# First attention chunks of a fused kernel: the diagonal bonus and the rounding remainder move to TensorE, the powers of the decay come from one scan

## The chip, the cores and the metric

One core of a Trainium2 chip runs the whole kernel. The metric is the device time of one execution in microseconds (us). The engines are TensorE (PE; PEld is its weight load), VectorE (DVE), ScalarE (ACT), GpSimd (POOL) and SyncE (SP), which here issues most DMAs. Each runs its own instructions in the order in which the program gives them, and waits on semaphores for the others.

## The reference

Three stages follow one another: a linear attention with a decay, a squared-ReLU MLP, and a mixture of experts that routes each token to two of eight. The change touches the first stage and what it hands to the second.

```python
B, H, S, D = r.shape                      # 4, 8, 768, 48
state = zeros(B, H, D, D)
for t in range(S):
    kt, vt, rt = k[:, :, t], v[:, :, t], r[:, :, t]
    cur = einsum('bhd,bhe->bhde', u[None] * kt, vt)
    y[:, :, t] = einsum('bhd,bhde->bhe', rt, state + cur)
    state = w[None, :, :, None] * state + einsum('bhd,bhe->bhde', kt, vt)
x = y.transpose(0, 2, 1, 3).reshape(3072, 384)
h = maximum(x @ w_in, 0); x = (h * h) @ w_out           # 384 -> 2048 -> 384
...
```

## The kernel before, in words

The 3072 tokens go in 24 chunks q of 128; four chunks make one block j of 512 tokens (TPB = 4, six blocks). A chunk of the attention has these steps. `load` brings r, k and v (192 KB each). `p_tr q r` and `p_tr q k` transpose r and k on TensorE, four transposes each, so that the head dimension lies on the partitions; for r, VectorE multiplies by powers of the decay on the way out of the bank (L444), for k of chunks 1 to 7, ScalarE copies (L448), since k was multiplied before (`pre_k`, L408). `pre q` makes r times k times u on GpSimd in two products (L395, L396), and `pre2 q` sums that over a head on VectorE (L414): dg, the bonus of the token itself, one number per token and head. ScalarE then writes am, eight diagonal matrices ident * dg (L419, eight instructions of 128x128). `p_a q` multiplies kT by rT (L459), and VectorE writes the part above the diagonal into am with a predicated copy (L463). `p_kv q` makes the state's update (L503; VectorE adds it to Z at L510, GpSimd multiplies by a power of the decay at L511). `p_y q 0` multiplies the old state, `p_y q 1` multiplies am by v, both into one bank (L477).

`p_x q` hands the chunk over: x1h = the bank rounded to the short fp32 format that TensorE multiplies in one pass (ScalarE, L522), x1l = bank - x1h, the remainder (VectorE, L523). mm1 then multiplies x1h and x1l by the halves of w_in (L540), nine matmuls per slice of 128 hidden units; gsplit squares and splits the result (L545 to L555), mm2 multiplies by w_out (L565, L571). For block 0, slice 0, the terms with x1l come last.

The weights w_in and w_out come in 16 pieces through two staging buffers (`load_w`). Piece n is split by `conv_w1` (ScalarE, L272), `conv_w2` part a and b (VectorE, L279 to L291), and `conv_w3` (ScalarE L301, GpSimd L302); the end of `conv_w2 n` issues the load of piece n+2.

The order of everything up to mm1 of block 0 is written out by hand in the tuple HEAD: each entry is a step, and the engines' queues get their instructions in that order. `warm n` are n transposes of the identity that nothing reads. Behind HEAD, the pieces of chunk 4 and later ones stand at fixed places between the 16 slices of mm1 and mm2 of the block before (CHUNKS: for chunk 4, pre2 at 0.83, p_kv at 1.23, p_y 0 at 1.96, p_a at 3.2, p_y 1 at 5.12; 2f is behind mm1 of slice f). Steps also issue DMAs on SP's queue: `pre q` loads k of q+2, `p_y q 1` v of q+2, `p_tr q k` (of chunk 4: r) r of q+2.

The powers T of the decay (one row per head dimension, centred on the middle of the chunk) are made ahead of HEAD on VectorE: a scan, the reciprocal of its middle column, and a second scan from there (L335 to L340). `tables` reverses them on ScalarE (L344), transposes them on TensorE (L347) and copies them out as tk (L348); `spread` writes u to all partitions by a matmul (L352) and a copy to ub (L354).

Banks of PSUM that the steps use are rings: "att" has three, "ph" two, "xo" one tile of three banks, and a new tile waits for the readers of the oldest released one.

Of the kernel before, what the change touches and what calls it, by code (L numbers as in the profile page):

```python
# [8 lines left out]
F32 = mybir.dt.float32  # L9
F32R = mybir.dt.float32r  # L10
BF = mybir.dt.bfloat16
I32 = mybir.dt.int32
AF = mybir.ActivationFunctionType
OP = mybir.AluOpType
AX = mybir.AxisListType
PSUM = bass.MemoryType.PSUM
DRAM = bass.MemoryType.DRAM
P = 128
# [5 lines left out]
OWN_ACT = 8  # L24
KP_POOL = (2, 3, 4, 5, 6, 7, 8)

HEAD = ("load_w 0", "p_tr 0 r", "spread", "pre 0", "p_tr 0 k", "warm 10", "tables", "pre2 0",
# [7 lines left out]

CHUNKS = (((0.72, 2.09, 0.63, 0.83, 1.23, 3.2, 1.96, 5.12, 6.53),
# [56 lines left out]
def body(ctx, tc, r, k, v, w, u, w_in, w_out, w_gate, w_noise, noise, w1, w2, out):  # L93
    nc = tc.nc
    B, H, S, D = r.shape
    DM = H * D
    FF = w_in.shape[1]
    E, _, F2 = w1.shape
    NT = B * S
    KD = DM // P  # L100
    NF = FF // P
    NF2 = F2 // P
    HP = H // 2
    NCH = NT // P
# [28 lines left out]
    C = {}  # L133
# [25 lines left out]
    ident = consts.tile([P, P], F32, name="ident")  # L159
# [16 lines left out]
    m1 = pool("m1", stack=c_ctx)  # L176
    at = pool("at", side="right", stack=a_ctx)
# [3 lines left out]
    QD = 2 * TPB  # L181
    SRC = {"r": r, "k": k, "v": v}

    def load(q, names="rkv"):
        if q >= NCH:
            return
        b, c = divmod(q, CPB)
        for nm in names:
            if nm in L.get(q, {}):
                continue  # L190
            if nm == "r" and q < QD:
                t = rp[q % 2][:, :, :D]
# [30 lines left out]
    wp = at.tile([P, HP], F32, name="wp")  # L223
# [96 lines left out]
    pb = bank()  # L320
    for _ in range(WARM):
# [5 lines left out]
    s0 = at.tile([P, HP, P], F32, name="s0", tag="rT", bufs=2)  # L327
    s1 = at.tile([P, HP, P], F32, name="s1", tag="rT", bufs=2)
    T = at.tile([P, HP, P], F32, name="pow")
    nc.vector.memset(s1, 0.0)  # L330
    nc.vector.memset(s1[:, :, :1], 1.0)
    nc.vector.tensor_copy(s0, wp[:, :, None].to_broadcast([P, HP, P]))
    nc.vector.memset(s0[:, :, :1], 0.0)
    flat = "p h n -> p (h n)"
    nc.vector.tensor_tensor_scan(T.rearrange(flat), s0.rearrange(flat), s1.rearrange(flat), 0.0,  # L335
                                 op0=OP.mult, op1=OP.add)
    wmid = at.tile([P, HP], F32, name="wmid")
    nc.vector.tensor_tensor(wmid, T[:, :, MID], T[:, :, MID], op=OP.mult)
    nc.vector.reciprocal(s1[:, :, :1], T[:, :, MID:MID + 1])
    nc.vector.tensor_tensor_scan(T.rearrange(flat), s0.rearrange(flat), s1.rearrange(flat), 0.0,  # L340
                                 op0=OP.mult, op1=OP.add)
    def tables():
        Tb = at.tile([P, HP, P], F32, name="back", tag="am", bufs=2)
        nc.scalar.activation(Tb, T[:, :, ::-1], AF.Copy)  # L344
        pb = bank()
        for hp in range(HP):
            nc.tensor.transpose(pb[:, hp * P:(hp + 1) * P], Tb[:, hp, :], ident)  # L347
        nc.scalar.activation(tk, pb.rearrange("p (h x) -> p h x", x=64)[:, :, :D], AF.Copy)  # L348
# [7 lines left out]
    def warm(n):  # L356
        pw = xops.tile([P, KD, BLK], F32, name="xo")
        for _ in range(n):
            nc.tensor.transpose(pw[:, 0, :P], ident, ident)

    Z = [at.tile([P, HP, 2 * D], F32, name=f"Z{i}") for i in range(2)]
    for t in Z:
        nc.gpsimd.memset(t, 0.0)
# [22 lines left out]
    def pre(q):  # L386
        a = A.setdefault(q, {})
        l = L[q]
        if q:
            pre_k(q)  # L390
        if q < QD:
            t = at.tile([P, H, D], F32, name="ra", bufs=2)
        else:
            t = at.tile([P, H, D], F32, name="rk", bufs=1)
        nc.gpsimd.tensor_mul(t, l["r"], l["k"])  # L395
        nc.gpsimd.tensor_mul(t, t, ub)  # L396
        a["rk"] = t
        load(q + 2, "k")
# [8 lines left out]
    def pre_k(q):  # L407
        (nc.gpsimd if q in KP_POOL else nc.vector).tensor_mul(kp[q % 2][:, :, :D], L[q]["k"], tk)  # L408

    def pre2(q):  # L410
        a, l = A[q], L[q]
        t = a["rk"]
        dg = at.tile([P, H], F32, name="dg", bufs=2)
        nc.vector.tensor_reduce(dg, t, axis=AX.X, op=OP.add)  # L414

        a["am"] = at.tile([P, H, P], F32, name="am", tag="am", bufs=2)
        if q < OWN_ACT:
            for h in range(H):
                nc.scalar.activation(a["am"][:, h, :], ident, AF.Copy, scale=dg[:, h:h + 1])  # L419
        else:  # L420
            nc.gpsimd.tensor_mul(a["am"], ident[:, None, :].to_broadcast([P, H, P]),
                                 dg[:, :, None].to_broadcast([P, H, P]))

        nc.gpsimd.tensor_copy(ends(q), pairs(q)[:, :, 32:64].rearrange("p a (s x) -> p a s x", s=2))

    def p_tr(q, which, *tag):
        a = A.setdefault(q, {})
        if q >= QD:
            t = a[which + "T"] = at.tile([P, HP, P], F32, name=which + "T", bufs=2)
            nc.vector.transpose(t.rearrange("p a (s i) -> p a i s", i=TQ),  # L430
                                turned[which].rearrange("p a (i x) -> p a i x", x=D)[:, :, :, :32])
            nc.gpsimd.tensor_mul(t[:KR], t[:KR], T[:KR] if which == "r" else T[:KR, :, ::-1])
            if which == "k":
                load_next(q + 1)
            return
        src = (rp if which == "r" else kp)[q % 2]
        pb = bank(*tag)
        for hp in range(HP):
            nc.tensor.transpose(pb[:KR, hp * P:(hp + 1) * P],
                                src.rearrange("p h x -> p (h x)")[:, hp * P:hp * P + KR], ident)  # L440
        t = at.tile([P, HP, P], F32, name=which + "T", bufs=2)
        src = pb[:KR].rearrange("p (h t) -> p h t", t=P)
        if which == "r":
            nc.vector.tensor_mul(t[:KR], src, T[:KR])  # L444
        elif q == 0:
            nc.vector.tensor_mul(t[:KR], src, T[:KR, :, ::-1])
        else:
            nc.scalar.activation(t[:KR], src, AF.Copy)  # L448
        if which == ("r" if q == TPB else "k"):
            if q + 2 < QD:  # L450
                load(q + 2, "r")
        a[which + "T"] = t

# [61 lines left out]
    def p_x(q, *tag):  # L515
        j, i = divmod(q, TPB)
        if i == 0:
            x1h[j] = m1.tile([P, KD, BLK], F32R, name="x1h", bufs=2)
            x1l[j] = m1.tile([P, KD, BLK], F32R, name="x1l", bufs=2)
        src = A[q]["y"][:, :DM].rearrange("p (d t) -> p d t", t=P)  # L520
        hi = x1h[j][:, :, i * P:(i + 1) * P]
        nc.scalar.activation(hi, src, AF.Copy)  # L522
        nc.vector.tensor_tensor(x1l[j][:, :, i * P:(i + 1) * P], src, hi.bitcast(F32), op=OP.subtract)  # L523
        if q + 1 == QD:
            load_next(QD)
        del A[q], L[q]
# [523 lines left out]
    def run(pieces, n):  # L1050
        for p in pieces[:n]:
# [1 line left out]
        del pieces[:n]  # L1053

    AW = 3
    steps = dict(spread=spread, warm=warm, p_tr=p_tr, pre=pre, tables=tables, pre_k=pre_k, load_w=load_w, p_a=p_a, pre2=pre2, p_kv=p_kv,
                 conv_w1=conv_w1, conv_w2=conv_w2, conv_w3=conv_w3, p_y=p_y, p_x=p_x, load=load)
    for step in HEAD:
        name, *args = step.split()
# [207 lines left out]
```

## Time and profile before

| | us |
|---|---|
| three runs | 954.05, 954.15, 956.12 (median 954.15) |
| the profiled execution | 954.55 |
| its span, first to last instruction | 952.8 |

The profile is of one execution; its times count from the first instruction of the span. A line of a timeline gives start, length, engine, line of the kernel, operation, output <- inputs, and in brackets the idle time ahead of it with what ended it. A line of a group gives the count, the busy time with the mean of one in ns, and the idle time ahead.

### The profile page before, as it was taken

What the parts mean: (1) busy time and instruction counts of PE and PEld (TensorE: products, weight loads), DVE (VectorE), ACT (ScalarE), POOL (GpSimd) and SP (SyncE); (2) the same over time, 40 slices, a digit from 0 to 9 for tenths busy, and PEclk for the clock granted to TensorE, in tenths of its full rate; (3) what the DMA queues carried; (4) which work ended last, traced back from release to release, by engine and by line L of the source; (5) the groups of instructions that cost most, each with busy time, mean ns of one, the idle gap of its engine ahead of it and who ended that gap; (6) DMA issues with size and microseconds to landing.
All of it is one profiled execution on the core that took longest, in us unless ns stands there. A gap on an engine that the chain in (4) does not pass through costs nothing.

```text
span 952.8 us, 17752 instructions
## 1 busy us (share of the span) xinstructions
PE 939.4 (99%) x6845; PEld 805.6 (85%) x6845; DVE 537.5 (56%) x982; ACT 432.7 (45%) x792; POOL 347.3 (36%) x406
## 2 busy tenths in 40 slices
PE   8899999999999999999999999999999999999997
PEld 7676787778778878877888899999989898989986
DVE  8999757635845563584254564554645555456420
ACT  5766655334534434453555542443444434444321
POOL 6665353544463372445030343122121221212112
PEclk9999999999999999999999999999999999999999
DMA  7655379932444271442024357476655555555212
GB/s 176 164 163 163 102 186 302 249 106 68 115 118 105 52 196 44 121 108 77 1 95 97 109 127 185 110 138 133 130 103 114 121 115 110 112 99 109 36 21 37
DMA packets 193233, 112.32 MB, mean 118 GB/s; under 512 B 131777, under 2 KB 185698, under 8 KB 193122
## 3 DMA queue, kind: packets, MB, share of 16 engines
q1 hardware_dynamic: 181698, 91.03, 37.9%
q0 software_dynamic: 10624, 19.74, 11.3%
q8 instruction: 75, 1.23, 0.6%
q14 instruction: 36, 0.29, 0.1%
q10 hardware_dynamic: 800, 0.02, 0.0%
HBM read 74.64 MB, written 36.12 MB: 116 GB/s over the span
## 4 chain that ended last, share of the span: by engine, by line
PE 92%; DVE 4%; DMA 1%; issue 1%; ACT 0%; POOL 0%; POOLq 0%; ACTq 0%; DVEq 0%; SPq 0%
PE ph L540 20%; PE ph L861 19%; PE xo L571 19%; PE y L918 14%; PE y L949 5%; PE att L477 4%; PE ph L949 2%; PE att L459 2%; PE att L604 2%; PE y L861 2%; PE xo L565 1%; PE att L962 1%; PE att L503 1%; DVE am L463 1%; DVE t L280 1%
## 5 line engine op out<-in xcount | busy, mean ns | idle before, releaser
L929 POOL DMA_INDIRECT out<-yt,id x56 | 87.2, 1556 | 297.4 <-ACT yt L927 256.7
L555 DVE TENSOR_TENSOR gl<-g,gh 128x512 fp32r<-128x512 f32 x90 | 77.7, 863 | 134.2 <-ACT gh L553 130.6
L904 DVE SCALAR_TENSOR_TENSOR hl<-ph,hh 128x512 fp32r<-128x512 f32 (+1 forms) x112 | 67.0, 599 | 113.1 <-ACT hh L903 112.2
L545 ACT ACTIVATE rt<-ph 128x512 f32<-128x512 f32 x96 | 57.1, 595 | 158.2 <-PE ph L540 138.5
L540 PE MATMUL ph<-x1h,wih 128*128 128x512 f32 x288 | 119.2, 414 | 0.0
L861 PE MATMUL ph<-xh,w0h 128*128 128x512 f32 (+3 forms) x336 | 118.0, 351 | 0.0
L861 PE MATMUL ph<-xl,w0h 128*128 128x512 f32 (+3 forms) x336 | 116.2, 346 | 0.0
L861 PE MATMUL ph<-xh,w0l 128*128 128x512 f32 (+3 forms) x336 | 116.2, 346 | 0.0
L540 PE MATMUL ph<-x1h,wil 128*128 128x512 f32 x288 | 112.5, 391 | 0.0
L540 PE MATMUL ph<-x1l,wih 128*128 128x512 f32 x288 | 112.2, 391 | 0.0
L571 PE MATMUL xo<-gh,wol 128*128 128x512 f32 x270 | 106.2, 393 | 0.0
L903 ACT ACTIVATE hh<-ph 128x512 fp32r<-128x512 f32 (+1 forms) x112 | 58.7, 525 | 88.9 <-PE ph L861 84.6
L918 PE MATMUL y<-w1h,hh 128*128 128x384 f32 x256 | 85.7, 335 | 0.0
L918 PE MATMUL y<-w1l,hh 128*128 128x384 f32 x256 | 85.6, 335 | 0.0
L918 PE MATMUL y<-w1h,hl 128*128 128x384 f32 x256 | 85.6, 334 | 0.0
L732 POOL DMA_INDIRECT sent<-row,si x48 | 50.2, 1045 | 63.7 <-DVE gl L555 44.8
L571 PE MATMUL xo<-gh,woh 128*128 128x512 f32 x180 | 71.6, 398 | 0.0
L571 PE MATMUL xo<-gl,woh 128*128 128x512 f32 x180 | 70.2, 390 | 0.0
L861 PEld LDWEIGHTS ph<-xh,w0l 128*128 128x128 f32 x336 | 63.2, 188 | 7.7
L861 PEld LDWEIGHTS ph<-xl,w0h 128*128 128x128 f32 x336 | 63.3, 188 | 7.6 <-DVE xl L830 0.8
L861 PEld LDWEIGHTS ph<-xh,w0h 128*128 128x128 f32 x336 | 63.3, 188 | 6.7
L540 PEld LDWEIGHTS ph<-x1h,wih 128*128 128x128 f32 x288 | 54.0, 188 | 16.3 <-issue 3.5
(234 smaller groups left out, 2143.3 us busy)
## 6 DMA issues: line engine op xcount, KB each, us to landing
ws<-in_moe_w SPq DMA_DIRECT2D x128, 96.0 KB
ws<-in_moe_w SPq DMA_DIRECT2D x32, 384.0 KB
sent<-zero SPq DMA_DIRECT2D x8, 1375.5 KB
G<-sent SPq DMA_DIRECT2D x36, 192.0 KB
stg<-in_moe_w_in SPq DMA_DIRECT2D x8, 768.0 KB
stg<-in_moe_w_out SPq DMA_DIRECT2D x8, 768.0 KB
out<-zero SPq DMA_DIRECT2D x5, 960.0 KB
lv<-in_v SPq DMA_DIRECT2D x24, 192.0 KB
```

What stands on the lines that cost most here:

```text
L477: nc.tensor.matmul(pb[32 * n:32 * n + 32, d, :], x, y, skip_group_check=True, **kw)
L540: nc.tensor.matmul(ph, wt[qi][:, d, sl], xt[j][:, d, :], start=(n == 0), stop=(n == 3 * KD - 1))
L545: nc.scalar.activation(rt, ph, AF.Relu)
L555: nc.vector.tensor_tensor(gl, g, gh.bitcast(F32), op=OP.subtract)
L571: nc.tensor.matmul(XO[j][:, d, :], wt[qi][:, fo, sl], gt, start=(f == 0 and n == 0), stop=(f == NF - 1 and n == 2))
L732: st = nc.gpsimd.indirect_dma_start(out=sent, in_=s["row"][:, i, :], in_offset=None, out_offset=bass.IndirectOffsetOnAxis(ap=s["si"][:, i, ...
L861: nc.tensor.matmul(ph[:, c], wt[:, d, sl], xt[:, d, c], start=(m == 0), stop=(m == 3 * KD - 1))
L903: nc.scalar.activation(hh[:, :n], ph, AF.Relu)
L904: nc.vector.scalar_tensor_tensor(hl[:, :n], ph, 0.0, hh[:, :n].bitcast(F32), op0=OP.max, op1=OP.subtract)
L918: nc.tensor.matmul(py, ht[:, sl], wt[:, fo, :], start=(m == 0), stop=(m == 3 * NF2 - 1))
L929: st = nc.gpsimd.indirect_dma_start(out=out, in_=yt, in_offset=None, compute_op=OP.add, out_offset=bass.IndirectOffsetOnAxis(ap=IDX[e, un] ...
L949: nc.tensor.matmul(py[d][:, c], wt[:, fo, sl], ht[:, c], start=(m == 0), stop=(m == 3 * NF2 - 1))
```

## The change

In chunks 1 to 4 (DOT) the bonus no longer comes from r, k and u: `dot q` multiplies kT by rT on GpSimd into rkT, and `pre2 q` multiplies rkT by uw (u times w, two columns per pair of heads) with four matmuls, and ScalarE copies the bank to dg. In chunks 0 to 3 `p_x` lets TensorE subtract x1h from the bank that holds the output (matmul with minus = -identity), and ScalarE copies what is left to x1l. The powers come from one scan, started at the reciprocal of w to the 64th, which six products and a reciprocal make; ScalarE writes the scan's factors. HEAD is put in another order, with `tables` in two parts, fewer `warm` transposes, and u loaded a second time in another layout.

```diff
-HEAD = ("load_w 0", "p_tr 0 r", "spread", "pre 0", "p_tr 0 k", "warm 10", "tables", "pre2 0",
-        "pre_k 0", "conv_w1 0", "pre 1", "p_tr 1 r", "pre2 1", "warm 2", "p_a 0", "p_kv 0",
-        "load 3 r", "load 2 r", "conv_w2 0 a", "p_tr 1 k", "p_y 0 0", "load_w 1", "warm 10",
-        "p_y 0 1", "p_tr 2 r", "pre 2", "p_kv 1", "p_x 0", "p_tr 2 k ph", "pre 3", "pre2 2",
-        "warm 10", "p_a 1", "p_y 1 0", "p_tr 3 r ph", "warm 4", "p_y 1 1", "conv_w2 0 b", "p_kv 2",
-        "p_x 1", "conv_w1 1", "conv_w3 0", "p_tr 3 k ph", "pre2 3", "p_a 2", "conv_w2 1 a",
-        "warm 9", "p_a 3 ph", "pre 4", "p_y 2 0", "p_y 2 1", "p_x 2", "conv_w1 2", "conv_w2 1 b",
-        "p_tr 4 r", "p_y 3 0", "p_kv 3", "p_y 3 1", "p_x 3", "conv_w3 1", "conv_w2 2", "p_tr 4 k")
+DOT = (1, 2, 3, 4)
+HEAD = ("load_w 0", "p_tr 0 r", "p_tr 0 k", "tables a", "spread", "pre 0", "tables b", "load 2 r",
+        "warm 10", "pre_k 0", "pre2 0", "conv_w1 0", "pre 1", "p_tr 1 r", "warm 2", "p_a 0",
+        "p_kv 0", "load 3 r", "p_tr 1 k ph", "dot 1", "conv_w2 0 a", "p_y 0 0", "load_w 1",
+        "warm 8", "p_y 0 1", "pre2 1", "p_tr 2 r", "pre 2", "p_kv 1", "p_x 0", "p_tr 2 k ph",
+        "dot 2", "pre 3", "warm 6", "p_a 1", "p_y 1 0", "pre2 2", "p_tr 3 r ph", "p_y 1 1",
+        "conv_w2 0 b", "p_kv 2", "p_x 1", "p_tr 3 k ph", "dot 3", "conv_w1 1", "conv_w3 0", "p_a 2",
+        "conv_w2 1 a", "warm 4", "pre2 3", "p_a 3 ph", "pre 4", "p_y 2 0", "p_y 2 1", "p_x 2",
+        "conv_w1 2", "conv_w2 1 b", "p_tr 4 r", "p_y 3 0", "p_kv 3", "p_y 3 1", "p_x 3", "conv_w3 1",
+        "conv_w2 2", "p_tr 4 k", "dot 4")
...
+    uc = at.tile([P, HP], F32, name="uc")
+    uw = at.tile([P, HP, 2], F32, name="uw")
+    nc.gpsimd.memset(uc, 0.0)
+    nc.gpsimd.memset(uw, 0.0)
...
     load(1)
+    for j in range(2):
+        nc.sync.dma_start(uc[64 * j:64 * j + D, :], u.rearrange("(p j) d -> j d p", j=2)[j])
     load(2, "k")
...
-    nc.vector.memset(s1[:, :, :1], 1.0)
-    nc.vector.tensor_copy(s0, wp[:, :, None].to_broadcast([P, HP, P]))
     nc.vector.memset(s0[:, :, :1], 0.0)
+    nc.scalar.activation(s0[:, :, 1:], wp[:, :, None].to_broadcast([P, HP, P - 1]), AF.Copy)
+    wmid = at.tile([P, HP], F32, name="wmid")
+    nc.vector.tensor_tensor(wmid, wp, wp, op=OP.mult)
+    for _ in range(MID.bit_length() - 2):
+        nc.vector.tensor_tensor(wmid, wmid, wmid, op=OP.mult)
+    nc.vector.reciprocal(s1[:, :, :1], wmid[:, :, None])
+    nc.vector.tensor_tensor(wmid, wmid, wmid, op=OP.mult)
     nc.vector.tensor_tensor_scan(T.rearrange(flat), s0.rearrange(flat), s1.rearrange(flat), 0.0,
                                  op0=OP.mult, op1=OP.add)
-    wmid = at.tile([P, HP], F32, name="wmid")
-    nc.vector.tensor_tensor(wmid, T[:, :, MID], T[:, :, MID], op=OP.mult)
-    nc.vector.reciprocal(s1[:, :, :1], T[:, :, MID:MID + 1])
-    nc.vector.tensor_tensor_scan(T.rearrange(flat), s0.rearrange(flat), s1.rearrange(flat), 0.0,
-                                 op0=OP.mult, op1=OP.add)
...
+    minus = m1.tile([P, BLK], F32R, name="minus", tag="rt", bufs=1)[:, :P]
+    nc.scalar.activation(minus, ident, AF.Copy, scale=-1.0)
...
     def pre(q):
...
             pre_k(q)
+        if q in DOT:
+            load(q + 2, "k")
+            return
...
+    def dot(q):
+        if q == DOT[0]:
+            for j in range(2):
+                rows = slice(64 * j, 64 * j + D)
+                nc.gpsimd.tensor_mul(uw[rows, :, j], uc[rows], wp[rows])
+        a = A[q]
+        t = a["rk"] = m1.tile([P, BLK], F32, name="rkT", tag="gl", bufs=3).rearrange("p (h t) -> p h t", t=P)
+        nc.gpsimd.tensor_mul(t[:KR], a["kT"][:KR], a["rT"][:KR])
...
     def pre2(q):
...
-        nc.vector.tensor_reduce(dg, t, axis=AX.X, op=OP.add)
+        if q in DOT:
+            pb = xops.tile([P, KD, BLK], F32, name="xo")[:, 0, :H] if q < TPB else bank()[:, :H]
+            for hp in range(HP):
+                nc.tensor.matmul(pb[:, 2 * hp:2 * hp + 2], t[:KR, hp, :], uw[:KR, hp, :], start=True, stop=True)
+            nc.scalar.activation(dg, pb, AF.Copy)
+        else:
+            nc.vector.tensor_reduce(dg, t, axis=AX.X, op=OP.add)
...
     def p_tr(q, which, *tag):
...
         if which == ("r" if q == TPB else "k"):
-            if q + 2 < QD:
+            if 0 < q < QD - 2:
                 load(q + 2, "r")
...
     def p_x(q, *tag):
...
         nc.scalar.activation(hi, src, AF.Copy)
-        nc.vector.tensor_tensor(x1l[j][:, :, i * P:(i + 1) * P], src, hi.bitcast(F32), op=OP.subtract)
+        lo = x1l[j][:, :, i * P:(i + 1) * P]
+        if q < TPB:
+            nc.tensor.matmul(src, minus, hi, start=False, stop=True, skip_group_check=True)
+            nc.scalar.activation(lo, src, AF.Copy)
+        else:
+            nc.vector.tensor_tensor(lo, src, hi.bitcast(F32), op=OP.subtract)
```

## Rows read from the trace of the kernel before

**Rows 1.** page: busy shares, slices of VectorE and of TensorE's clock, one costly group

```profile
PE 939.4 (99%) x6845; PEld 805.6 (85%) x6845; DVE 537.5 (56%) x982; ACT 432.7 (45%) x792; POOL 347.3 (36%) x406
...
DVE  8999757635845563584254564554645555456420
...
PEclk9999999999999999999999999999999999999999
...
L918 PE MATMUL y<-w1h,hh 128*128 128x384 f32 x256 | 85.7, 335 | 0.0
```

**Rows 2.** page: chain that ended last, shares by engine

```profile
PE 92%; DVE 4%; DMA 1%; issue 1%; ACT 0%; POOL 0%; POOLq 0%; ACTq 0%; DVEq 0%; SPq 0%
```

**Rows 3.** waits of TensorE from 33 us to the end: us in total, times, longest

```profile
PE att L459 <- DVE Z L510: 1.0, 1, 1.0
PE att L477 <- DVE am L463: 0.8, 3, 0.4
PE att L477 <- issue: 0.8, 2, 0.5
PE att L503 <- DMA lv<-in_v: 0.6, 1, 0.6
```

**Rows 4.** timeline of TensorE, first two slices of mm1: start, us

```profile
33.22 0.50 PE L540 MATMUL ph<-x1h,wih 128*128 128x512 f32 x1
...
37.60 0.50 PE L540 MATMUL ph<-x1h,wih 128*128 128x512 f32 x1
```

**Rows 5.** timeline of VectorE, 4 to 36 us

```profile
4.22 1.23 DVE L335 TENSOR_TENSOR_SCAN pow<-s,s 128x512 f32<-128x512 f32 x1
...
5.77 1.96 DVE L340 TENSOR_TENSOR_SCAN pow<-s,s 128x512 f32<-128x512 f32 x1
...
19.73 0.56 DVE L523 TENSOR_TENSOR x1l<-att,x1h 128x384 fp32r<-128x384 f32 x1
...
20.20 0.54 DVE L414 TENSOR_REDUCE dg<-ra 128x8 f32<-128x384 f32 x1
...
35.44 2.08 DVE L280 TENSOR_SCALAR t<-t 128x768 int32<-128x768 int32 x1
```

**Rows 6.** timeline of ScalarE, 10 to 26 us

```profile
10.48 2.43 ACT L419 ACTIVATE am<-ident,dg 128x128 f32<-128x128 f32 x8
...
13.71 0.93 ACT L272 ACTIVATE t<-stg 128x768 f32<-128x768 f32 x1 [0.79 <-DMA stg<-in_moe_w_in]
...
14.54 2.44 ACT L419 ACTIVATE am<-ident,dg 128x128 f32<-128x128 f32 x8
...
16.89 0.58 ACT L448 ACTIVATE kT<-att 112x512 f32<-112x512 f32 x1
...
17.37 0.47 ACT L522 ACTIVATE x1h<-att 128x384 fp32r<-128x384 f32 x1
...
20.84 2.45 ACT L419 ACTIVATE am<-ident,dg 128x128 f32<-128x128 f32 x8 [2.52 <-DVE dg L414]
...
25.70 2.44 ACT L419 ACTIVATE am<-ident,dg 128x128 f32<-128x128 f32 x8
```

**Rows 7.** timeline of TensorE, 1 to 30 us

```profile
1.84 4.10 PE L322 MATMUL att<-ident 128*128 128x128 f32 x18 [1.84 <-POOL ident masks.py:199]
...
8.37 1.25 PE L359 MATMUL xo<-ident 128*128 128x128 f32 x10
...
13.26 0.62 PE L439 MATMUL att<-ident,kp 128*112 128x128 f32 x4 [0.98 <-DVE rT L444]
...
29.64 0.86 PE L477 MATMUL att<-rT,Z 112*32 112x128 f32 x24
```

**Rows 8.** timeline of SP's queue

```profile
1.00 0.87 SPq L234 DMA_DIRECT2D wp<-in_w  x2
```

**Rows 9.** instructions of tile kT: duration ns min/median/max

```profile
L432 POOL TENSOR_TENSOR kT<-kT,pow x16: 1283/1293/1998, 131.5 to 432.0; 112x512 f32<-112x512 f32 x16
```

**Rows 10.** groups of GpSimd instructions by form

```profile
L302 POOL TENSOR_TENSOR wil<-t,wih 128x768 fp32r<-128x768 f32 x8 | 15.6, 1946 | 23.2 <-ACT wih L301 22.9
```

More of the change, by code (lines that the diff above doesn't have):

```diff
@@ L336, in body, with tables @@
                                  op0=OP.mult, op1=OP.add)
-    wmid = at.tile([P, HP], F32, name="wmid")
-    nc.vector.tensor_tensor(wmid, T[:, :, MID], T[:, :, MID], op=OP.mult)
-    nc.vector.reciprocal(s1[:, :, :1], T[:, :, MID:MID + 1])
-    nc.vector.tensor_tensor_scan(T.rearrange(flat), s0.rearrange(flat), s1.rearrange(flat), 0.0,
-                                 op0=OP.mult, op1=OP.add)
-    def tables():
-        Tb = at.tile([P, HP, P], F32, name="back", tag="am", bufs=2)
-        nc.scalar.activation(Tb, T[:, :, ::-1], AF.Copy)
+    def tables(part):
+        if part == "a":
+            C["back"] = at.tile([P, HP, P], F32, name="back", tag="am", bufs=2)
+            nc.scalar.activation(C["back"], T[:, :, ::-1], AF.Copy)
+            return
+        Tb = C.pop("back")
         pb = bank()
@@ L390, in pre @@
             pre_k(q)
+        if q in DOT:
+            load(q + 2, "k")
+            return
         if q < QD:
@@ L1055, in body @@
     AW = 3
-    steps = dict(spread=spread, warm=warm, p_tr=p_tr, pre=pre, tables=tables, pre_k=pre_k, load_w=load_w, p_a=p_a, pre2=pre2, p_kv=p_kv,
+    steps = dict(dot=dot, spread=spread, warm=warm, p_tr=p_tr, pre=pre, tables=tables, pre_k=pre_k, load_w=load_w, p_a=p_a, pre2=pre2, p_kv=p_kv,
                  conv_w1=conv_w1, conv_w2=conv_w2, conv_w3=conv_w3, p_y=p_y, p_x=p_x, load=load)
```

## The prediction, made before the changed kernel was run

> **What bounds it now.** The busy shares come first: TensorE 99%, and a granted clock of nine tenths or more in every slice [rows 1]. The chain that ended last, followed back from the last instruction, says the same: 92% TensorE [rows 2]. So nothing is won by making another engine shorter; the time changes only if TensorE's stream of products starts earlier or later, or has holes. Next come the waits of TensorE behind 33 us: 3.2 us in all, 0.6 of them before 37.6 us [rows 3]. Its timeline gives the marks: the first product of the first linear layer (mm1 for block 0, slice 0) starts at 33.22 us, the second slice's at 37.60 [rows 4]. Everything that the change touches lies ahead of 37.60 or just behind. Two tenths of a per cent, 1.9 us, is about what a measurement of this kernel can tell from no change.
>
> Then the question is what ends last before 33.22. VectorE is full there: two scans, three reduces and four remainders that the change takes out (one scan of the two, three of the reduces), and tensor_scalar instructions that are drawn out, to 2.08 us at 35.44, while GpSimd multiplies [rows 5]. ScalarE is less full: it makes am of one chunk after the other at 14.54, 20.84 and 25.70 [rows 6], each 2.4 us, and can do am 1 **ahead of** kT 1 and kT 2, since the bonus comes from r, k and u on GpSimd and hangs on no transposed tile.
>
> **Part 1, one scan.** Out: one scan (1.23) and the copy s0, which goes to ScalarE. In: eight small VectorE instructions; the two that stand between the scans now fill 0.32 (5.45 to 5.77), so 0.16 to 0.2 each where one waits for the other, 1.5 in all. The one scan starts near 4.9 and the powers are there near 6.1 instead of 7.73 [rows 5]. But the transposes of r 0 end near 6.7, since four take 0.62 and stand behind the 18 warm-up transposes that end at 5.94 [rows 7], so rT 0 gains 1.0. tk gains some 1.5 in the same way. am 0 gains nothing: its bonus still goes over spread, ub and two GpSimd products, so it starts near 10.5 as now (10.48) [rows 6].
>
> **Part 2, DMA issues.** Two transfers of u, of the shape of wp's two, whose issue took 0.87 for both, stand on SP's queue ahead of load(2,"k") and the first weight piece [rows 8]. That piece's landing releases conv_w1 0 at 13.71 [rows 6]. Bounds: 0 (the engines are busy anyway) and 0.9 (all the issue time); I take 0.4, in the middle: conv_w1 0 at 14.1, done at 14.95, kT 1 behind it on ScalarE at 15.55. Load 2 r keeps its place behind load_w 0. The later loads wait on fewer readers; what is asked of them comes later.
>
> **Part 3, the bonus by TensorE.** Removed per chunk: two GpSimd products and a reduce, 0.47 from its start to the next [rows 5]. Added: one GpSimd product of 112x512 (the same shape: 1.28 to 2.0, median 1.29 [rows 9]; I take 1.35), four matmuls of two columns (not in this trace; below, one matmul's 0.27, above, 0.9; I take the 0.62 of four transposes, which load as many weights [rows 7]), and a ScalarE copy of 128x8 (not in this trace; at most the 0.30 of a 128x128 step of am, below, half of it; I take 0.25) [rows 6]. The prices are small; the **order** is not. The product needs kT, so am(q) now stands behind kT(q), and HEAD puts x1h(q-1) behind am(q) on ScalarE.
>
> **Part 4, the remainder by TensorE.** Removed: four VectorE subtractions of 0.47 from start to start [rows 5]. Added: a matmul of 384 columns (a row of as many columns has 0.335 [rows 1]; between 0.27 and 0.5, I take 0.45 where another engine waits for it, 0.35 in TensorE's own order) and a ScalarE copy of 0.47, like x1h [rows 6]. The matmul waits for x1h(q-1), which is behind am(q), and TensorE takes its instructions in order: queued behind it are p_tr(q+1) k, p_a(q) and p_y(q) 0. And p_tr(q+1) k is what the next kT comes from.
>
> So parts 3 and 4 together close a **loop** that runs once per chunk and has no work to overlap with: kT 0.58, product 1.35, four matmuls 0.62, copy 0.25, am 2.44, x1h 0.47, subtracting matmul 0.45, transposes of the next k 0.62, and eight hand-overs of about 0.04 (0.3): 7.1 us. Now am 1 to am 3 start 5.6 apart on average (14.54 to 25.70) [rows 6], and not by such a loop.
>
> **The sum.** kT 1 ends at 15.55, kT 2 at 22.6, kT 3 at 29.7; conv_w1 1 and conv_w3 0 (1.8 on ScalarE) lie beside the product and matmuls of chunk 3. Product, matmuls, copy and am 3 take 4.8: am 3 ends at 34.5 (now 28.1 [rows 6]). From there TensorE's order holds: x1h 2 0.47, its matmul 0.35, p_tr 4 r 0.46 (0.62 without its tail, as every block that another follows), p_y 3 0 0.7 and p_y 3 1 1.1 (24 of its small matmuls take 0.86 with the tail, 32 a third more [rows 7]), p_kv 3 near 0.5, x1h 3 0.5, its matmul 0.35, p_tr 4 k 0.46: mm1 starts at 39.4 instead of 33.22, +6.2. VectorE, relieved of some 3.8 (1.0, and six times 0.47), waits in that time.
>
> A second hole follows. pre2 4 stands behind mm1 slice 0 (at 0.83 in block 0), and its four matmuls wait for dot 4, the last of HEAD on GpSimd, behind wil of conv_w3 1 (1.95 on average [rows 10]). That one follows lo 3 and wih on ScalarE: 39.6, 40.4, 42.4; dot 4, with conv_w2 2 beside it nearer 1.7, ends at 44.1. mm1 slice 0 is through at 41.7. After matmuls, p_kv 4 and p_y 4 0 (0.6, 0.5, 0.7, with hand-overs) slice 1 starts near 46.2 instead of 37.60: +8.6. Behind that the other engines are ahead of TensorE, and the 2.6 us of waits that lie behind 37.60 [rows 3] go: +6.0. No wait of TensorE is left later to take anything back. On the profiled execution of 954.55 this gives 960.5; the median of the runs shown lies 0.4 below it: **960.0**, rounded. The weight pieces don't matter: VectorE's part of them moves by less than TensorE.
>
> Bounds: with 0.27 for the matmuls, 0.15 for the copy, 0.27 for the subtraction, 1.29 for the product and no later landing, a turn is 6.1 and the sum +2.5: 956.6. With 1.75 for the product, 0.9, 0.30, 0.5 and a landing 0.9 late it is +9: 963.1. That is this case's own range.
>
> **The rivals.** (a) **VectorE was the bound and its relief shows.** For it: VectorE is busy eight, nine and nine tenths of the first three slices of 24 us [rows 1], and 1.0 of scan with 2.8 of three reduces and three remainders (the fourth is not waited for) leave it, so mm1 would start 3.8 earlier: 950.3. It needs am(q) to be ready when p_a(q) is, that is a loop below 5.6 us; against it stands that am, x1h, kT and the product alone are 4.8 and two hand-overs to TensorE come on top. (b) **It cancels.** If ScalarE or GpSimd run a turn in 5.6 to 6.2, mm1 slice 1 is late by about what the waits of [rows 3] give back: 953 to 956. (c) **TensorE's clock falls.** TensorE would have holes of 1.3 to 3 us where now the longest in the head is 0.98 [rows 7]. The first 18 transposes took 228 ns each, later ten started 109 apart (1.25 with the last one's 0.27 through) [rows 7], though the clock's first slice is as full as the others; at the first pace the 1.7 us of TensorE in a turn double, and so does part of the stretch behind the wait for dot 4: 2 to 5 us more, 962 to 965. Against it: the granted clock is full in each slice with the holes there are [rows 1]. [...] (d) That the remainder is not formed would not change the time.
>
> **How the numbers follow.** The forecast has 0.68, (a) 0.12, (b) 0.09, (c) 0.11. (a) gives faster, (b) mostly same, the others slower. The range reaches from the upper half of (b) to most of (c): 955.5 to 964.5; with (a) and the rest of (b) and (c) that leaves out 0.2.
>
> **What would show it.** Right: am 1, 2, 3 on ScalarE about 7 us apart and starting near 18, 25 and 32; TensorE waiting for x1h (minus <- x1h) and for GpSimd's rkT; mm1 first near 39, second slice near 46; VectorE idle for several us before 40. Wrong: mm1 near 30 with am ahead of kT, the products done beside other work; or a granted clock below 1 in 12 to 48 us, which would speak for (c).

## The result, and the profile after

The changed kernel takes 968.22 us (median of four executions, 967.92 to 970.95); the kernel before, beside it, 954.38. The ratio is 1.0143 [1.013, 1.0157]: slower by 13.8 us, in the predicted direction and 3.7 us past the upper end of the range. The profiled execution of the changed kernel is the longest of its four (970.95, span 969.2; the others lie between 967.92 and 968.35), so its marks can lie later than those of the median.

The page of the changed kernel, the lines that answer to [rows 1] and [rows 2]:

```profile
PE 950.6 (98%) x6866; PEld 816.2 (84%) x6866; DVE 536.5 (55%) x977; ACT 436.7 (45%) x802; POOL 342.4 (35%) x406
...
DVE  5688866555663683576253375554554545456420
...
PEclk8789999999999999999999999999999999999999
...
PE 96%; POOL 1%; DMA 1%; ACT 1%; issue 0%; SPq 0%; DVE 0%; POOLq 0%; ACTq 0%
```

VectorE is down by three tenths in its first and second slices and by one in its third and fourth. The line below it is the surprise: the granted clock of TensorE is 8, 7 and 8 tenths in the first three slices, where it was 9 in each. TensorE's busy time grew by 11.2 us: the new bonus matmuls alone fill some 6.5 of it (four groups of 1.05 to 1.87), and products that both kernels have take longer at the lower clock (the first of slice 1, below: 0.80 for 0.50).

The waits of TensorE from 5 us on (engine, tile and line <- what it waited for: total us, times, longest):

```profile
PE att L442 <- POOL rkT L433: 3.2, 1, 3.2
PE xo L442 <- POOL rkT L433: 2.8, 2, 2.3
PE att L556 <- ACT x1h L553: 2.6, 3, 1.4
```

These are the two kinds of wait that the change adds: the bonus matmuls for GpSimd's product, and the subtracting matmul for x1h. They make 8.6 us, against 13.8 us of loss; over the same stretch all waits of the kernel before make 4.6.

The timeline of ScalarE, against [rows 6]:

```profile
3.40 1.28 ACT L340 ACT_TABLE_LOAD   x1 [3.40 <-DMA wp<-in_w]
...
15.32 0.91 ACT L280 ACTIVATE t<-stg 128x768 f32<-128x768 f32 x1 [1.68 <-DMA stg<-in_moe_w_in]
16.12 0.59 ACT L479 ACTIVATE kT<-ph 112x512 f32<-112x512 f32 x1
...
20.27 2.44 ACT L450 ACTIVATE am<-ident,dg 128x128 f32<-128x128 f32 x8
...
31.46 2.45 ACT L450 ACTIVATE am<-ident,dg 128x128 f32<-128x128 f32 x8
...
39.23 2.45 ACT L450 ACTIVATE am<-ident,dg 128x128 f32<-128x128 f32 x8
```

am 1 to am 3 start at 20.27, 31.46 and 39.23 (14.54, 20.84 and 25.70 before): 11.2 and 7.8 us apart, where the prediction had 7.1. The first weight piece, at the second line, is 1.6 us later than in [rows 6], not 0.4. (That mark scatters: the same loads ahead of it gave 14.10 to 15.32 in eight profiles here, and this one is the latest.)

The timeline of TensorE, with the first products of mm1 slices 0 and 1 as the third and the last line, against [rows 4]; then GpSimd's product of chunk 2:

```profile
18.16 1.87 PE L442 MATMUL xo<-uw,rkT 112*128 112x2 f32 x8 [2.31 <-POOL rkT L433]
...
29.34 1.87 PE L442 MATMUL xo<-uw,rkT 112*128 112x2 f32 x8
...
46.50 0.48 PE L576 MATMUL ph<-x1h,wih 128*128 128x512 f32 x1
...
52.05 1.71 PE L442 MATMUL att<-uw,rkT 112*128 112x2 f32 x8 [3.23 <-POOL rkT L433]
...
55.76 0.80 PE L576 MATMUL ph<-x1h,wih 128*128 128x512 f32 x1
```

```profile
25.46 1.26 POOL L433 TENSOR_TENSOR rkT<-kT,rT 112x512 f32<-112x512 f32 x1 [2.12 <-ACT kT L479]
```

Slice 0 starts 13.3 us later and slice 1 18.2 us later. The profiled execution is 16.4 us longer, so the whole loss is there by 56 us, and 1.8 us of slice 1's delay are taken back behind it. Windows of the changed kernel show why (stretch, length; busy us and count of PE, PEld, DVE, ACT, POOL; granted clock, DMA share, GB/s):

```profile
12.00:60.00 48.00, 38.95 (x542) 32.10 (x541) 31.70 (x39) 25.89 (x65) 21.73 (x22) 0.75 0.54 132
16.00:18.00 2.00, 0.00 (x0) 0.00 (x0) 1.71 (x2) 0.71 (x2) 1.16 (x1) 1.00 0.95 171
18.00:20.00 2.00, 1.84 (x9) 1.84 (x10) 1.49 (x2) 0.00 (x0) 2.00 (x3) 0.53 1.03 349
20.00:30.00 10.00, 8.62 (x91) 7.00 (x91) 2.75 (x5) 4.09 (x12) 3.83 (x6) 0.50 0.36 71
34.00:36.00 2.00, 2.00 (x44) 1.57 (x35) 0.71 (x2) 1.13 (x3) 0.70 (x2) 0.70 0.66 129
50.00:52.00 2.00, 0.00 (x0) 0.00 (x0) 2.00 (x2) 1.74 (x4) 2.00 (x3) 1.00 0.41 62
52.00:60.00 8.00, 7.95 (x81) 6.42 (x82) 6.52 (x7) 3.50 (x11) 3.23 (x4) 0.57 0.29 101
```

The same stretches of the kernel before:

```profile
12.00:60.00 48.00, 44.30 (x621) 34.19 (x609) 45.44 (x63) 31.11 (x69) 31.52 (x30) 1.00 0.66 173
20.00:30.00 10.00, 9.92 (x218) 8.34 (x219) 9.62 (x15) 8.09 (x22) 9.69 (x11) 1.00 0.67 164
```

Twice TensorE has nothing for 2 us (16 to 18, 50 to 52), and each time the granted clock is about half right behind it (0.53 from 18 to 20 us, 0.57 from 52 to 60). Behind the first hole it stays there to about 35 us (0.50 from 20 to 30, 0.70 on average from 34 to 36). In 20 to 30 us TensorE is busy for 8.62 us with 91 products, where the kernel before does 218 in 9.92. In those 10 us VectorE is busy for 2.75 instead of 9.62. That is more than the work taken from it: it now waits for the others, and its relief is of no use.

### The profile page after: what moved, and what is told of

Its sections match the earlier page's. It is cut to its first block, busy times and chain, and to the rows that moved or that the text cites. A ratio compares the mean times of both kernels' runs of the same rounds, so it can differ in the third digit from the quotient of the medians.

```text
span 969.2 us, 17809 instructions
## 1 busy us (share of the span) xinstructions
PE 950.6 (98%) x6866; PEld 816.2 (84%) x6866; DVE 536.5 (55%) x977; ACT 436.7 (45%) x802; POOL 342.4 (35%) x406
## 4 chain that ended last, share of the span: by engine, by line
PE 96%; POOL 1%; DMA 1%; ACT 1%; issue 0%; SPq 0%; DVE 0%; POOLq 0%; ACTq 0%
PE ph L576 21%; PE xo L607 19%; PE ph L897 19%; PE y L954 13%; PE y L985 5%; PE att L508 4%; PE att L490 2%; PE ph L985 2%; PE att L640 2%; PE y L897 2%; PE xo L601 2%; PE att L998 1%; PE att L534 1%; DMA stg<-in_moe_w_in 1%; PE xo L442 0%
## 5 line engine op out<-in xcount | busy, mean ns | idle before, releaser
L591 DVE TENSOR_TENSOR gl<-g,gh 128x512 fp32r<-128x512 f32 x90 | 83.4, 927 | 134.7 <-ACT gh L589 128.5
L576 PEld LDWEIGHTS ph<-x1h,wih 128*128 128x128 f32 x288 | 54.4, 189 | 16.4 <-issue 3.1
```

Source lines behind the costliest of these rows:

```text
L576: nc.tensor.matmul(ph, wt[qi][:, d, sl], xt[j][:, d, :], start=(n == 0), stop=(n == 3 * KD - 1))
L591: nc.vector.tensor_tensor(gl, g, gh.bitcast(F32), op=OP.subtract)
```

## The experiments

Theory: the changed order makes a loop without overlap, worth some 8 us, and its holes let the clock fall, which costs as much again. Rivals: the order alone costs it all; the u loads do; the remainder's place alone does; the scan does. Chips differ by up to 2.7 us (the kernel before took 952.39 to 955.04), so the ratios to the kernel before on the same chip are compared.

**Fill the holes with idle transposes.** The order of the computing steps stays; only transposes of the identity that nothing reads are added ahead of what waits (the lines of HEAD are shown in part, as in the cuts below).

```diff
-        "warm 8", "p_y 0 1", "pre2 1", "p_tr 2 r", "pre 2", "p_kv 1", "p_x 0",
+        "warm 8", "p_y 0 1", "warm 12", "pre2 1", "p_tr 2 r", "pre 2", "p_kv 1", "warm 20", "p_x 0",
...
-        "conv_w2 0 b", "p_kv 2", "p_x 1",
+        "conv_w2 0 b", "p_kv 2", "warm 12", "p_x 1",
...
-        "warm 4", "pre2 3", "p_a 3 ph", "pre 4", "p_y 2 0", "p_y 2 1", "p_x 2",
+        "warm 4", "warm 6", "pre2 3", "p_a 3 ph", "pre 4", "p_y 2 0", "p_y 2 1", "warm 6", "p_x 2",
...
-        "p_y 3 1", "p_x 3",
+        "p_y 3 1", "warm 6", "p_x 3",
...
     def pre2(q):
+        if q == DOT[-1]:
+            warm(24)
```

> The changed kernel with idle transposes (warm) put into TensorE's holes, ahead of the instruction that waits: 62 in HEAD and 24 ahead of chunk 4's bonus matmuls. Order of all other work unchanged. Theory (the order makes a loop of about 7 us per chunk, and the holes it leaves let the clock fall, which costs as much again): granted clock 1.00 from 12 to 60 us, am 1 to am 3 start about 7.4 apart, mm1 starts near 41.6 and its second slice near 48.5, time 961 to 963. Rival A (the clock alone is the loss; the order is nearly free): 954 to 957. Rival B (the clock's fall costs little, the rest is new waits and contention): 966 or more.

Measured: 960.25 us beside 952.40, ratio 1.0084 [1.0067, 1.0101]. Its windows, and marks of its timelines of ScalarE, GpSimd and TensorE:

```profile
12.00:60.00 48.00, 47.09 (x699) 40.01 (x689) 36.75 (x46) 31.09 (x73) 27.81 (x26) 1.00 0.61 149
20.00:30.00 10.00, 10.00 (x162) 8.92 (x162) 3.75 (x7) 5.97 (x19) 4.39 (x7) 1.00 0.51 91
```

```profile
14.42 0.94 ACT L281 ACTIVATE t<-stg 128x768 f32<-128x768 f32 x1 [0.94 <-DMA stg<-in_moe_w_in]
...
18.61 2.45 ACT L453 ACTIVATE am<-ident,dg 128x128 f32<-128x128 f32 x8
...
26.14 2.46 ACT L453 ACTIVATE am<-ident,dg 128x128 f32<-128x128 f32 x8
...
33.92 2.45 ACT L453 ACTIVATE am<-ident,dg 128x128 f32<-128x128 f32 x8
```

```profile
23.14 1.27 POOL L434 TENSOR_TENSOR rkT<-kT,rT 112x512 f32<-112x512 f32 x1 [2.15 <-ACT kT L482]
```

```profile
24.04 0.86 PE L511 MATMUL att<-rT,Z 112*32 112x128 f32 x24
...
24.83 1.05 PE L445 MATMUL xo<-uw,rkT 112*128 112x2 f32 x8
...
41.19 0.48 PE L579 MATMUL ph<-x1h,wih 128*128 128x512 f32 x1
...
48.40 0.50 PE L579 MATMUL ph<-x1h,wih 128*128 128x512 f32 x1
```

Work that computes nothing brings back 0.59% (1.0143 less 1.0084), 5.6 us; by the two intervals, taken as independent, between 3.5 and 7.7. The clock is full, and the loop is still there: am 1 to am 3 are 7.5 and 7.8 us apart. What is left, 0.84% or 8.0 us, is the order's. One of the fills costs a little itself: ahead of chunk 3's bonus the transposes end 0.6 us after the product, so the order alone is nearer 7.4 (an estimate: it takes the 0.6 to reach the end).

**Only the first hole, and only the last.** The first kernel keeps of these fills only "warm 12" ahead of "pre2 1", the second only the 24 ahead of chunk 4's bonus.

```diff
-        "warm 8", "p_y 0 1", "pre2 1",
+        "warm 8", "p_y 0 1", "warm 12", "pre2 1",
```

> The changed kernel with 12 idle transposes in one place, the first long hole of TensorE (ahead of chunk 1's bonus matmuls, where it did nothing from 15.8 to 18.2 us). Theory: that hole makes the clock fall at 18.1, and the half-clock stretch of 17 us that follows goes or starts later, at the next hole ahead of the first subtracting matmul: ratio to the kernel before 1.010 to 1.013 (the changed kernel: 1.0143, filled everywhere: 1.0084). Rival (any of the holes does it, filling one is worth nothing): 1.0135 to 1.016, with a half-clock stretch of 10 us or more still ahead of 40.

```diff
     def pre2(q):
+        if q == DOT[-1]:
+            warm(24)
```

> The changed kernel with 24 idle transposes in one place, ahead of chunk 4's bonus matmuls behind mm1's first slice, where TensorE waited 3.2 us. Theory: the second half-clock stretch (52.2 to 59.1, over dense matmuls) goes, the first one (18.1 to 35.2) stays; half of 6.8 us less: ratio 1.0100 to 1.0115. Rival (the second stretch comes from something else than that hole): 1.0135 or more, with a half-clock stretch between 50 and 60 still there.

The first: 968.77 beside 955.04, ratio 1.0151 [1.0133, 1.0168]: no gain at all, as the rival had it. The second: 966.05, ratio 1.0111 [1.0093, 1.013]. Windows of the first, then of the second:

```profile
20.00:22.00 2.00, 0.17 (x1) 0.17 (x1) 0.54 (x2) 1.77 (x6) 1.00 (x2) 0.96 0.61 120
22.00:24.00 2.00, 2.00 (x9) 1.91 (x10) 0.00 (x0) 1.09 (x2) 0.00 (x0) 0.50 0.64 112
```

```profile
20.00:32.00 12.00, 10.38 (x91) 8.85 (x95) 2.98 (x5) 4.90 (x17) 3.46 (x5) 0.51 0.27 52
50.00:60.00 10.00, 9.40 (x106) 7.74 (x107) 9.77 (x11) 8.22 (x18) 6.19 (x7) 1.00 0.40 122
```

With the first hole cut from 2.31 to 1.0 us, the clock falls at the next one (2.15 us, for x1h): TensorE busy for 0.17 of 2 us, and half the clock right behind (0.50 from 22 to 24). So it is not that one hole that makes the clock fall: the loop leaves others that do. The last hole, filled alone, keeps 50 to 60 us at the full clock and is worth 0.32% (3 us; by the two intervals 0.9 to 5.2).

**The remainder back to VectorE**, the bonus by TensorE kept (minus, no longer needed, goes too): once as it is, once with fills. The fills stand where this kernel has its holes, 12, 5, 6 and 10 transposes in HEAD and 22 ahead of chunk 4's bonus, so they are not those of the filled kernel above.

```diff
-        if q < TPB:
+        if False:
             nc.tensor.matmul(src, minus, hi, start=False, stop=True, skip_group_check=True)
```

> The changed kernel with the remainder x1l subtracted by VectorE again in all chunks; the bonus by TensorE, the scan and HEAD as changed. Theory: the transposes of the next k no longer wait behind x1h, a turn is 6.2 instead of 7.4, mm1 starts near 37.7 at full clock, second slice near 44.8 (the hole ahead of chunk 4's bonus stays, 2.7 us): 959 to 961 if the clock stays full, 962 to 965 if it falls in that hole or before. Rival (the subtracting matmul has no part in it): within 1.5 us of the changed kernel.

> The remainder by VectorE (as e2) and idle transposes in TensorE's holes (as e1): both taken together, at full clock. Theory (the loop is kT, product, matmuls, copy, am, x1h, subtracting matmul, transposes of the next k; without the subtracting matmul in TensorE's order a turn is 6.2 instead of 7.5): granted clock 1.00 from 12 to 60, am 2 and am 3 about 6.2 apart, mm1 starts near 37.7 (e1: 41.2), ratio to the kernel before 1.004 to 1.006 (e1: 1.0084, e2: 1.0071). Rival (the loop is set by the bonus alone): am starts still 7 or more apart, ratio 1.0075 or more.

Measured: as it is 958.29, ratio 1.0071 [1.005, 1.0092], granted clock 0.93 in 12 to 60 us; filled 957.47, ratio 1.0052 [1.0037, 1.0067], clock 1.00. The timeline of ScalarE of the filled one:

```profile
19.29 2.45 ACT L451 ACTIVATE am<-ident,dg 128x128 f32<-128x128 f32 x8
...
25.91 2.45 ACT L451 ACTIVATE am<-ident,dg 128x128 f32<-128x128 f32 x8
...
32.55 2.45 ACT L451 ACTIVATE am<-ident,dg 128x128 f32<-128x128 f32 x8
```

With both at the full clock a turn goes from 7.5 and 7.8 to 6.6 us (6.2 was expected) and the time down by 0.32% (3 us; by the two intervals 0.9 to 5.2). So the subtracting matmul stands in the loop. It costs 0.9 us in the first turn and, without the 0.6 of the other kernel's fill, some 0.5 in the second.

**The remainder alone.** On the kernel before, with the one scan (see below), p_x subtracts by TensorE in chunks 0 to 3; the bonus is the old one.

```diff
-        nc.vector.tensor_tensor(x1l[j][:, :, i * P:(i + 1) * P], src, hi.bitcast(F32), op=OP.subtract)
+        lo = x1l[j][:, :, i * P:(i + 1) * P]
+        if q < TPB:
+            nc.tensor.matmul(src, minus, hi, start=False, stop=True, skip_group_check=True)
+            nc.scalar.activation(lo, src, AF.Copy)
```

> The kernel of e8 (one scan, bonus by the old way, order as in the kernel before) with the remainder of chunks 0 to 3 by TensorE, where p_x stands: part 4 alone. Theory: TensorE, in order, waits 0.7 to 1.5 us for each x1h where VectorE's subtraction let it go on, and banks stay taken until the copy; VectorE's relief of 2 us is not seen: mm1 starts near 36 (e8: 33.2), ratio 1.0010 to 1.0025 at full clock, up to 1.006 if the clock falls. Rival (VectorE bounds the head, its relief is worth its 2 us): 0.998 or less.

Measured: 954.54 beside 952.39, ratio 1.0024 [1.0014, 1.0033]. A line of its waits of TensorE, and a window:

```profile
PE att L531 <- ACT x1h L528: 3.1, 4, 1.6
```

```profile
20.00:30.00 10.00, 9.72 (x214) 8.39 (x211) 7.70 (x13) 7.76 (x21) 8.79 (x10) 1.00 0.74 170
```

Here am comes from r, k and u, so no loop closes, and TensorE stays busy at the full clock (9.72 of 10 us at 1.00). The matmul's own waits for x1h still make it slower, though VectorE has 1.9 us less to do in 20 to 30 than before. mm1 starts at 35.12 (33.19 with the one scan alone). That is the moved remainder by itself: 0.24%, 2.3 us lost. The bonus by itself, filled, lost 0.52% (above); the two make 0.76%, beside the 0.84% of both in the filled kernel.

**Chunk 4's bonus the old way**, on the filled kernel.

```diff
-DOT = (1, 2, 3, 4)
+DOT = (1, 2, 3)
...
-        "p_x 3", "conv_w3 1", "conv_w2 2", "p_tr 4 k", "dot 4")
+        "p_x 3", "conv_w3 1", "conv_w2 2", "p_tr 4 k")
```

> The filled kernel (e1) with chunk 4's bonus by GpSimd products and a VectorE reduce again (DOT = 1, 2, 3; no filling ahead of chunk 4). Theory: the hole of 3 us between mm1's first two slices goes, of which 1.5 us reach the end, since the small waits behind it come back: mm1 starts at 41.2 as in e1, second slice near 45, ratio 1.0060 to 1.0075 (e1: 1.0084). Rival (that wait is hidden or only moved): 1.0080 or more.

Measured: 958.23, ratio 1.0068 [1.0052, 1.0084]. The first products of slices 0 and 1 in its timeline of TensorE:

```profile
41.26 0.48 PE L577 MATMUL ph<-x1h,wih 128*128 128x512 f32 x1
...
44.64 0.50 PE L577 MATMUL ph<-x1h,wih 128*128 128x512 f32 x1
```

Slice 1 is 3.8 us earlier than in the filled kernel. The end is 0.16% (1.5 us) earlier, but the intervals overlap, so a gain there is not shown. It is the second hole of the prediction, and most of what it costs at slice 1 seems to be taken back behind it.

**The u loads later**, and ScalarE's first table load earlier, on the filled kernel.

```diff
     load(1)
-    for j in range(2):
-        nc.sync.dma_start(uc[64 * j:64 * j + D, :], u.rearrange("(p j) d -> j d p", j=2)[j])
...
     def load_w(n):
...
+        for j in range(0 if n else 2):
+            nc.sync.dma_start(uc[64 * j:64 * j + D, :], u.rearrange("(p j) d -> j d p", j=2)[j])
...
+    minus = m1.tile([P, BLK], F32R, name="minus", tag="rt", bufs=1)[:, :P]
+    nc.scalar.activation(minus, ident, AF.Copy, scale=-1.0)
     s0 = at.tile([P, HP, P], F32, name="s0", tag="rT", bufs=2)
```

> The filled kernel (e1) with u's second load issued behind the first weight piece, and minus made ahead of s0 on ScalarE, so that its table load no longer waits for w. Theory: the first piece lands near 13.9 instead of 15.2, the scan starts 0.4 earlier, am 1 starts 0.5 to 1.4 earlier and everything behind it: ratio 1.0065 to 1.0080 (e1: 1.0084). Rival (the u transfers cost nothing): within 0.0004 of e1.

Measured: 962.08 beside 955.04, ratio 1.0072 [1.0055, 1.0089]. Two lines of its timeline of ScalarE:

```profile
0.83 1.28 ACT L337 ACT_TABLE_LOAD   x1 [0.83 <-PEq L1292]
...
13.86 0.94 ACT L281 ACTIVATE t<-stg 128x768 f32<-128x768 f32 x1 [0.94 <-DMA stg<-in_moe_w_in]
```

The first weight piece comes 0.56 us earlier than in the filled kernel (14.42), the scan starts at 4.89 instead of 5.37, and the two slices of mm1 at 40.62 and 47.82, 0.57 and 0.58 earlier. One pair of profiles says little of the piece, since it scatters: used at 14.10 to 15.32 in the eight profiles with u ahead of it, at 13.29 to 13.86 in the five without (the kernel before among them). So u delays it, by more than the 0.4 of the prediction in most of them. The run moves two things at once and can't tell them apart at mm1; at the end the intervals overlap, and a gain there is not shown.

**One scan alone.** The kernel before with the new powers and the changed first steps.

```diff
-HEAD = ("load_w 0", "p_tr 0 r", "spread", "pre 0", "p_tr 0 k", "warm 10", "tables", "pre2 0",
+HEAD = ("load_w 0", "p_tr 0 r", "p_tr 0 k", "tables a", "spread", "pre 0", "tables b", "warm 10",
...
```

> The kernel before with one scan in place of two and the changed kernel's order of the first steps (tables in two parts, kT 0 ahead of spread); bonus and remainder as before, no second load of u. Theory: am 0 still waits for ub and two products, so next to nothing reaches mm1: 953.5 to 954.6, no change. Rival (the scan is on the path, VectorE's front bounds): 952.5 to 953.3, about 1 us faster.

Measured: 959.96, ratio 1.0079 [1.0062, 1.0096], a miss that came from the edit. p_tr 0 k, now ahead of pre 0, still issued the load of chunk 2's r, and the products of chunk 0 waited for it and took it: in this run the bonus of chunk 0 is made from chunk 2's r. The line of GpSimd's timeline:

```profile
14.13 0.99 POOL L399 TENSOR_TENSOR ra<-rp,kp 128x384 f32<-128x384 f32 x1 [10.01 <-DMA rp<-in_r]
```

Repeated with that load behind chunk 0's products, as the change has it, and with an early ScalarE instruction that takes the table load:

```diff
+        "load 2 r", "warm 10", "pre_k 0", "pre2 0",
...
-            if q + 2 < QD:
+            if 0 < q < QD - 2:
                 load(q + 2, "r")
```

> The kernel before with one scan and the changed order of the first steps, this time with load 2 r behind the products of chunk 0 as in the changed kernel (in e4, p_tr 0 k issued it ahead of them, so they waited for chunk 2's r and multiplied it), and with the table load of ScalarE early. Theory: am 0 hangs on ub and two products, so next to nothing reaches mm1: ratio 0.9990 to 1.0005. Rival (the scan was on the path): 0.9985 or less.

Measured: 954.60 beside 955.04, ratio 0.9994 [0.9985, 1.0004], and mm1 at 33.19 (33.22 before). One scan fewer is worth nothing. A wait of TensorE and a window:

```profile
PE att L465 <- DVE Z L516: 1.7, 1, 1.7
```

```profile
40.00:44.00 4.00, 2.62 (x17) 2.23 (x18) 3.87 (x7) 4.00 (x11) 3.45 (x4) 0.74 0.55 203
```

Slice 1 of mm1 starts at 36.90, 0.7 us earlier than in the kernel before, and this is lost again: chunk 4's p_a waits for VectorE's Z to 41.38 (41.36 before), a wait of 1.7 us where it was 1.0 [rows 3], and here the clock falls behind it (0.74 from 40 to 44 us, 1.00 before).

**The old bonus in the new order** (DOT empty, no dot steps).

```diff
-DOT = (1, 2, 3, 4)
+DOT = ()
```

> The changed kernel with the bonus of chunks 1 to 4 by two GpSimd products and a VectorE reduce again; the remainder by TensorE, the scan and HEAD as changed without the dot steps. Theory: am no longer stands behind kT, am 1 starts near 16.7, am 2 near 21.2; what stays is TensorE waiting 2.4 us for x1h 0 in order; mm1 starts near 37, second slice near 40.5: 956 to 957 at full clock, up to 960 if the clock falls. Rival (the bonus has no part, the blocking matmul is all): within 2 us of the changed kernel.

Measured: 967.20, ratio 1.0152 [1.0135, 1.0169], a miss. A line of VectorE's timeline and one of TensorE's:

```profile
18.68 0.54 DVE L445 TENSOR_REDUCE dg<-ra 128x8 f32<-128x384 f32 x1
```

```profile
22.19 0.69 PE L556 MATMUL att<-x1h,minus 128*128 128x384 f32 x1 [5.39 <-ACT x1h L553]
```

The new order has pre2 behind conv_w2, where TensorE's matmuls had to stand; VectorE's reduce inherits that place and is late too. It is no clean undoing of part 3, and the clock falls here too (0.82 from 12 to 60 us). The run says only that this order, with either bonus, makes TensorE wait for x1h.

**A later place for chunk 4's p_a and p_y 1**, on the one-scan kernel, in search of a faster one.

```diff
-CHUNKS = (((0.72, 2.09, 0.63, 0.83, 1.23, 3.2, 1.96, 5.12, 6.53),
+CHUNKS = (((0.72, 2.09, 0.63, 0.83, 1.23, 4.2, 1.96, 6.4, 6.53),
```

> The kernel of e8 with chunk 4's p_a one slice later (4.2 in place of 3.2) and its p_y 1 at 6.4 in place of 5.12, so that TensorE does not wait for VectorE's update of Z and its predicated copy (1.7 and some 1.0 us in e8). If these waits go and nothing behind them is late: ratio 0.9975 to 0.9985. Rival (the waits only move, or p_x 4 makes others late): 0.999 to 1.001.

Measured: 961.07 beside 952.39, ratio 1.0087 [1.0074, 1.0101], a miss. A wait of TensorE, and VectorE's line that ends it:

```profile
PE att L483 <- DVE am L469: 10.6, 1, 10.6
```

```profile
56.54 1.33 DVE L469 COPY_PREDICATED am<-mask,att 128x512 f32<-128x512 uint16 x2
```

The predicated copy came to stand behind weight pieces on VectorE, which is busy with them from 47.3 to 56.5, and the clock falls with that wait (0.58 from 50 to 60). No version here beats the kernel before; the one-scan kernel equals it.

## Why the prediction was right in direction and wrong in size

- **What bounds the kernel** was right. Only the start and the holes of TensorE's stream count: slice 1 is 18.2 us late and the end 16.4.
- **Part 1** was right: nothing gained at mm1 or at the end (the one-scan run). The scan started at 5.35, not 4.9, because the load of ScalarE's table (1.28 us from 3.40) stood behind the wait for w.
- **Part 2** was undersized: the issue of the two u loads took 1.47 us, not 0.87, and the first weight piece was used at 14.42 (filled) or 15.32, for 14.1. At mm1 this and the table load together are worth 0.57.
- **Part 3** had the order right and one price outside its bounds: four matmuls of two columns took 1.05 us at the full clock (0.62 taken, at most 0.9). The copy took 0.18 for 0.25, the product 1.27 to 1.29 for 1.35 in chunks 1 to 3, and 2.00 for 1.7 in chunk 4.
- **Part 4, the loop,** is what happened: 7.1 us predicted, 7.5 and 7.8 measured at the full clock. The matmuls' 0.4 are in each turn; in one 0.4 more comes from p_y 1 0, which holds TensorE till 24.83 though the product was done at 24.41, and 0.6 in the other from the fill; the rest of the terms came out some 0.4 smaller in all. Taking the subtracting matmul out gave 6.6. (The turn of 6.1 at the lower bound leaves out the eight hand-overs; with them its own terms make 6.4.)
- **The sum** for the order was +6.0, with mm1 at 39.4 and slice 1 at 46.2; the filled kernel has 41.19, 48.40 and +8.0. Of the 1.8 us at mm1 some 0.7 were there at am 1 (18.61 for near 18) and 1.1 came from two turns (33.92 less 18.61 is 15.3, for 14.2). Slice 1 is 10.8 late and the end 8.0: the 2.8 taken back answer to the 2.6 of waits that were to go. At the ratio 1.0084 that would be 962.4, inside the forecast's own range (956.6 to 963.1).
- **The step that failed is the choice against rival (c).** The sum has no term for the clock: it takes all products at the full pace through the holes, and (c), with a chance of 0.11, was set aside because "the granted clock is full in each slice with the holes there are". But behind the start the longest waits there were 1.0 us [rows 3, 7], and the prediction itself had worked out holes of up to 3 us. Rows of the kernel before could not speak for such holes; the argument took them as if they did. In the changed kernel the granted clock is 0.50 from 20 to 30 us (with TensorE busy for 8.62 of the 10) behind a hole of 2.31 us, and it is 1.00 in 12 to 60 once idle transposes fill the holes. The pace of the first 18 transposes (228 ns), which the prediction brought for (c), is no evidence for it: the trace gives the clock as full (1.00) from 2 to 6 us, and what slowed them is open.
- **The price in (c)** was 2 to 5 us, and 5.6 measured, with 3.5 to 7.7 open; so it may have been low, and its time, 962 to 965, was 3.2 us short also because the order was. It counted the 1.7 us of TensorE in each turn. At half the clock (0.50 from 20 to 30 us) other products counted as well: GpSimd's product of chunk 2 was done at 26.72, but its bonus matmuls stood in TensorE's order behind idle transposes, p_a 1 and p_y 1 0 and started at 29.34, and that turn took 11.2 us where the filled kernel has 7.5. Behind dot 4 the half clock (0.57 from 52 to 60) cost part of the 3 us that the fill there brought back. That order (8.0) and clock (5.6) make up the result is no check: the second is the result less the first.
- **Rival (a)** is excluded: in the filled kernel, with the clock full, VectorE is idle for 6.25 of the 10 us from 20 to 30, and a turn still takes 7.5. **(b)** fell with the same turn. **(d)** is no matter of time; the matmul with minus is in the trace in each of chunks 0 to 3.

## What to carry to other kernels

Taking work off a busy engine wins nothing if what replaces it stands in another engine's queue behind a result that comes late: write down the loop from that result back to itself, and compare one turn with the spacing before the change. Where such a loop leaves TensorE idle as long as here (2.31 and 3.23 us), count the loss twice, once for the hole and once for the slower products behind it (granted clock 0.50 and 0.57), and don't take a full clock over short holes (1.0 us here) as evidence for long ones. Idle transposes in the holes separate the two costs in one run (8.0 and 5.6 us here).

## What the runs showed of the hardware

- In the changed kernel the clock fell behind a hole of 2.31 us and stayed near half for some 17 us (0.50 from 20 to 30) though TensorE was busy for 8.62 of those 10. With holes filled by transposes that nothing reads it was 1.00 from 12 to 60 us. Filling one hole of several moved the fall to the next (0.50 in 22 to 24) and gained nothing. In the one-scan kernel it fell behind a wait of 1.7 us (0.74 from 40 to 44); with the remainder alone, the longest wait was 1.6 us and it stayed at 1.00 from 12 to 60. With the last hole alone filled it was still 1.00 from 18 to 20 behind a wait of 1.87 us, so these runs show no one length at which it falls.
- Four matmuls with weights of 112x128 and two moving columns (eight instructions) took 1.05 us at the full clock (1.00) and 1.87 at half (0.50): as small as the operands are, they cost more than four 128x128 transposes (0.62, [rows 7]).
- In the changed kernel the load of ScalarE's table (1.28 us) came at 3.40, behind the DMA of w; with an instruction in front that does not use w it ran at 0.83. In the kernel before it ran at 0.84, though the first instruction behind it came only at 7.99.
- Two small loads of u in another layout took 1.47 us to issue ahead of the weight piece and 0.91 behind it. With them ahead on SP's queue the piece was used at 14.10 to 15.32 (eight profiles), without at 13.29 to 13.86 (five).
